# Plain float32 products in the first token block, weight splits after the last conversion, and a new order of the attention's small products

## The chip, the cores and the metric

The kernel runs on one core of a Trainium2 chip. The metric is device microseconds (us) from start to end of one execution: 2131.81 us is the median of three runs of the kernel before (2130.74 to 2133.03).

## The reference, cut to what matters

Three layers run one behind the other on 4 sequences of 768 tokens (3072 tokens, 384 features).

```python
# 1. gated linear attention, 8 heads of 48: for every token t
state = f[t][:, None] * state + outer(k[t], v[t])     # f = sigmoid(f_logit)
y[t] = q[t] @ state
# 2. first MoE (one dense expert), w_in 384 x 2048, w_out 2048 x 384; weights arrive as float64
x2 = square(maximum(y @ w_in, 0)) @ w_out
# 3. second MoE: 8 experts of width 1024, Sinkhorn-normalised gates P (8 rounds)
out = sum(P[:, e:e+1] * (maximum(x2 @ w1[e], 0) @ w2[e]) for e in range(8))
```

All results are float32. A product of two float32 matrices can be made in two ways on TensorE: "plain", with both operands as float32; or "split", where each operand is cut into a rounded part (type float32r, `hi`) and a rest (`lo = a - hi`), and three float32r products hi·hi, hi·lo and lo·hi are added up in PSUM.

## The kernel before, in words

Tokens are worked in 24 chunks of 128 (`c`), three chunks to a block of 384 (`blk` for attention, `j` for the first MoE), eight blocks. The first MoE has 16 slices `f` of 128 hidden features. Its step number is `i = 16 j + f`.

**Attention, per chunk.** Scans over the forget gates on DVE (`scan_r`, `scan_f`, L316 to L325), products with k and q on POOL (`mul_k` L328, `mul_q` L331), scores on TensorE (`scores` L344), the causal mask on DVE (L349), transposition and state update (`k_turn` L354, `state_in` L366), and the output `y` (`mix`): for each of four pairs of heads `p`, two products of the masked scores with v (L383; 128 rows, 64 columns of the array each, the left half for head `j=0`, the right for `j=1`), and, except for the first chunk of a sequence, two products of the old state with q (L386; rows and columns 64j to 64j+63 of the array). The order is pair after pair, L383 L383 L386 L386. All of them write one PSUM bank. ACT then copies `y` to the hi part of `x1` (`yh`, L417), DVE makes the lo part (`yl`, L415). In block 0 the fourth pair's output is spread to the other three by a product with a shift matrix (L404).

**Weights of the first MoE.** Each of the 16 slices comes from memory as 128 x 768 float64 words (`ldw`, into one of four buffers) and is converted to float32 by `cva` and `cvw` on ACT (L930, L933), three `cvb` steps on DVE (L937, L941, L945) and `cvs` on POOL (L949). Right behind that it is split: `cvh` on ACT (L280) writes the hi part, `cvl` (L283) the lo part, on DVE for ten of the slices and on POOL for six. A conversion buffer (`cvt`, three of them) is free again after `cvl`.

**First MoE, per step i.** `e1` (L499): nine float32r products of 128x128 by 128x384 (three feature tiles, three terms each). ACT: `r` (relu, L504), `sq` (square, L507), `hi` (L511). DVE: `lo` (L515). Then `e2` (L525): nine float32r products into three accumulators. `e2(i)` is due two steps behind `e1(i)`. Two PSUM buffers hold the results of `e1`, so `e1(i)` needs `r(i-2)`.

**Order.** Nothing is ordered by hand: `Plan.order` (L65 on) is a list scheduler. Every step has an engine, a cost in us, a due time in units of `i`, and the steps that it needs. The result is one order per engine, and each engine runs its queue strictly in that order. Conversions are due at `n - 4` and start no earlier than 14 + 3.5 n us of the planner's own clock. While no work is there at the start, `keep_warm` fills TensorE with products of the identity matrix (L245).

The second MoE follows (L678 first products, L729 second products); its prepared weights rotate through the ten slots of `wpool`, which before held slices 0 to 9 of the first MoE.

Of the kernel before, what the change touches and what calls it, by code (L numbers as in the profile page):

```python
# [20 lines left out]
NP = H // 2  # L21
# [32 lines left out]
LO_DVE = (4, 6, 8, 9, 10, 11, 12, 13, 14, 15)  # L54
# [96 lines left out]
def body(tc, fkq, v, wm, wa, wc, gate, seqs, out):  # L151
# [5 lines left out]
    wpool = ctx.enter_context(tc.tile_pool(name="wpool", bufs=NWP))  # L157
# [23 lines left out]
    wb = rpool("wb", NF - NWP)  # L181
# [82 lines left out]

    def new_w(n):
        W[n] = (wb if n >= NWP else wpool).tile([128, 2, WCOL], F32R, tag="w", name="w")
        return W[n]

    def ldw(n):
        if n in early:  # L270
            early[n] = early[n - 4] if n >= 4 else wb.tile([128, WCOL], I64, tag="w", name="raw64")
        raws[n] = early[n] if n in early else rawp.tile([128, WCOL], I64, tag="raw", name="raw64")
        sp.dma_start(out=raws[n], in_=wm[n])
# [101 lines left out]
    def new_y(c):  # L375

        tmp["y", c] = (ps_p if c >= CPB else ps_acc).tile([128, NP, CH], F32, tag="pp" if c >= CPB else f"a{1 + c % 2}", name="y")

    def mix_pair(c, p, rows=64):
        y, vv, kk, st = tmp["y", c], vt[c % 3], kq[c % 3], Sh.get(c)  # L380
# [3 lines left out]
        if st is not None:  # L384
            for j in range(2):
                pe.matmul(y[64 * j:64 * j + rows, p, :], st[64 * j:64 * j + DH, p, 0:rows], kk[64 * j:64 * j + DH, 1, p, :], start=False, stop=True)  # L386

    def mix(c):
        new_y(c)
        for p in range(NP):  # L390
            mix_pair(c, p)
        Psb.pop(c)


    def mix_last(c):
        new_y(c)
        mix_pair(c, NP - 1)

    def last_out(c):
        act.copy(out=ylast, in_=tmp["y", c][:, NP - 1, :])  # L400

    def mix_rest(c):
        for p in range(KD):
            pe.matmul(tmp["y", c][:, p, :], shift[:, 16 * p:16 * p + 128], ylast, start=True, stop=True)  # L404
            mix_pair(c, p, DH)
        Psb.pop(c)

    def y_part(c, lo):
        blk, t0 = c // CPB, (c % CPB) * CH
        if blk not in x1:  # L410
            x1[blk] = x1p.tile([128, 2, NP, BT], F32R, tag="x1", name="x1")
        n = NP if blk else KD
        hi, y = x1[blk][:, 0, 0:n, t0:t0 + CH], tmp["y", c][:, 0:n, :]
        if lo:
            dve.tensor_tensor(out=x1[blk][:, 1, 0:n, t0:t0 + CH], in0=y, in1=hi.bitcast(F32), op=ALU.subtract)  # L415
        else:
            act.copy(out=hi, in_=y)  # L417
# [7 lines left out]
    for c in range(NCH):  # L425
# [40 lines left out]
        needs = [("cm0", c), ("cm1", c), ("ldv", c), if_(not first, ("sh", c)), if_(1 < c < CPB, ("yl", c - 2))]  # L466
        if blk:
            at("mix", "pe", 2.1 if not first else 1.1, 2.5, mix, needs)
# [6 lines left out]
        at("yl", "dve", 0.62 if blk else 0.5, 3, lambda c: y_part(c, 1), [("yh", c)])  # L475
# [13 lines left out]
    add("conv", "none", 0, 0, close_conv, [("cvl", n) for n in range(NF)])  # L489
# [4 lines left out]
    def products_in(i, w, xx):  # L494
        ps = eps[i] = ps_e.tile([128, BT], F32, tag="e1", name="e1")
        n = 0
        for k in range(KD):
            for wl, xl in ((0, 0), (0, 1), (1, 0)):
                pe.matmul(ps, w[:, wl, k * 128:(k + 1) * 128], xx[:, xl, k, :], start=n == 0, stop=n == 3 * KD - 1)  # L499
                n += 1  # L500

    def m_relu(i):
        hl[i] = [hp.tile([128, BT], F32, tag="g", name="g", bufs=2)]
        act.activation(out=hl[i][0], in_=eps.pop(i), func=ACTF.Relu)  # L504
# [12 lines left out]
    def m_out(i):  # L517
        j, f = divmod(i, NF)
        _, hi, lo = hl.pop(i)
        w = W[f]  # L520
        if f == 0:
            acc1[j] = [ps_acc.tile([128, BT], F32, tag=f"a{m}", name=f"a{m}") for m in range(KD)]
        for m in range(KD):
            for n, (wl, g) in enumerate(((0, hi), (1, hi), (0, lo))):
                pe.matmul(acc1[j][m], w[:, wl, D + m * 128:D + (m + 1) * 128], g, start=f == 0 and n == 0, stop=f == NF - 1 and n == 2)  # L525
        if j == NB - 1:
            W.pop(f)
# [17 lines left out]
    E1, E2 = 1.49, 1.49  # L545
# [4 lines left out]
    for i in range(n1):  # L550
        j, f = divmod(i, NF)
        add(("e1", i), "pe", E1, i, lambda i=i: products_in(i, W[i % NF], x1[i // NF]),
            [("yl", q) for q in range(CPB) if i == 0] + [if_(j == 0, ("cvl", f)), if_(f == 0 and j, ("sprd", j)), if_(i, ("e1", i - 1)), e_free(i)])
        add(("r", i), "act", 0.42, i + 0.4, lambda i=i: m_relu(i), [("e1", i), if_(i >= 2, ("lo", i - 2))])
        add(("sq", i), "act", 0.45, i + 0.4, lambda i=i: m_square(i), [("r", i)])
        add(("hi", i), "act", 0.45, i + 0.4, lambda i=i: m_hi(i), [("sq", i), if_(i >= 3, ("e2", i - 3))])
        add(("lo", i), "dve", 0.5, i + 0.4, lambda i=i: m_lo(i), [("hi", i)])
        add(("e2", i), "pe", E2, i + LAG + 0.1, lambda i=i: m_out(i),
# [235 lines left out]
    for g in range(NSTEP):  # L794
# [125 lines left out]
class F64:  # L920
# [79 lines left out]
def general_path(ctx: ExitStack, tc: tile.TileContext, seqs, wm, wa, wc, gate, out):  # L1000
# [27 lines left out]
    with tc.tile_pool(name="g_a", bufs=2) as ap, tc.tile_pool(name="g_s", bufs=3) as sp_, \  # L1028
            tc.tile_pool(name="g_y", bufs=2 * hb, space=PSUM) as py, tc.For_i(0, B, 1) as b:
        for p in range(NP):  # L1030
# [17 lines left out]
            for h in range(hb):  # L1048
                t = ap.tile([128, BT], F32, name="g_yo")
                act.copy(out=t, in_=y[h])  # L1050
                for j in range(2):
                    if p < KD:
                        sp.dma_start(out=x1v[bass.ds(b, 1), h, 64 * j:64 * j + DH, p].rearrange("o p t -> (o p) t"), in_=t[64 * j:64 * j + DH, :])
                    else:
                        for kt in range(KD):
                            sp.dma_start(out=x1v[bass.ds(b, 1), h, 64 * j + DH:64 * j + 64, kt].rearrange("o p t -> (o p) t"),
                                         in_=t[64 * j + 16 * kt:64 * j + 16 * kt + 16, :])
# [85 lines left out]
def lay_out(inputs):  # L1143
# [16 lines left out]
    for kt in range(KD):  # L1160
        rows += [2 * kt * DH + r for r in range(DH)]
        rows += [6 * DH + 16 * kt + r for r in range(16)]
        rows += [(2 * kt + 1) * DH + r for r in range(DH)]
        rows += [7 * DH + 16 * kt + r for r in range(16)]
# [27 lines left out]
```

## Time and profile before

| | |
|---|---|
| median of 3 runs | 2131.81 us |
| profiled execution | 2132.19 us |
| its span (first to last instruction) | 2130.4 us |
| TensorE busy / granted clock over the span | 98% / 0.990 of full speed |
| DVE, ACT, POOL busy | 62%, 42%, 30% |

The span and the profiled execution's time differ by 1.8 us. Busy shares are averages over very different stages: attention and first MoE run to about 590 us, the second MoE from there to the end. So the views of single stretches count here, not the averages.

### The profile page before, as it was taken

The page shows a single profiled execution, that of the slowest core. Times are in us where ns is not written, and L with a number is a line of the kernel's source. Part 1 is how long each engine was busy: PE and PEld are TensorE (multiplying, and loading weights), DVE is VectorE, ACT ScalarE, POOL GpSimd, SP SyncE. Part 2 cuts the span into 40 slices and gives each one's busy share as a digit, 9 for nine tenths or more (in the row PEclk, how much of TensorE's full clock was granted, in tenths as well). Part 3 has the DMA queues.
Part 4 walks back from the last instruction along what each step waited for, and adds up shares of the span by engine and source line. Part 5 has one row for each costly group of instructions (what it writes and reads, how often), then busy time and mean ns, then how long its engine had stood idle before and what let it go on. Part 6 is the DMA issues. An engine that isn't in the chain of part 4 may idle for free.

```text
span 2130.4 us, 27837 instructions
## 1 busy us (share of the span) xinstructions
PE 2080.0 (98%) x10686; PEld 1762.8 (83%) x10686; DVE 1325.2 (62%) x2022; ACT 886.4 (42%) x1505; POOL 638.1 (30%) x636
## 2 busy tenths in 40 slices
PE   7889999999999999999999999999999999999998
PEld 5789899998987888878878888888887888888886
DVE  8973443332477666657677666756767766766674
ACT  4754444454643433423434433433433433443341
POOL 4531100010103333333332333334233243333331
PEclk9899999999999999999999999999999999999999
DMA  7342212110203111112122112121213111211210
GB/s 269 127 128 65 77 67 83 57 49 7 81 31 91 55 55 60 55 55 70 55 86 88 55 55 70 55 62 52 68 62 108 61 59 52 69 55 55 70 45 32
DMA packets 55114, 148.76 MB, mean 70 GB/s; under 512 B 6332, under 2 KB 15548, under 8 KB 54972
## 3 DMA queue, kind: packets, MB, share of 16 engines
q1 hardware_dynamic: 54972, 146.90, 21.6%
q8 instruction: 85, 1.39, 0.3%
q14 instruction: 57, 0.47, 0.1%
HBM read 135.28 MB, written 9.54 MB: 68 GB/s over the span
## 4 chain that ended last, share of the span: by engine, by line
PE 90%; DVE 6%; issue 1%; DMA 1%; POOL 1%; ACT 0%; SPq 0%; DVEq 0%; POOLq 0%; ACTq 0%
PE o L729 35%; PE e L678 33%; PE e L499 9%; PE a L525 8%; PE y L383 1%; PE y L386 1%; PE pp L344 1%; DVE cv_t L937 1%; DVE cv_t L945 1%; PE lg L540 1%; DVE lo L515 1%; PE ds L366 0%; DVE cv_t L941 0%; DVE w L283 0%; DVE sg L318 0%
## 5 line engine op out<-in xcount | busy, mean ns | idle before, releaser
L729 PE MATMUL o<-h,w 128*128 128x512 f32 x3456 | 792.8, 389 | 0.0
L729 PEld LDWEIGHTS o<-h,w 128*128 128x128 f32 x3456 | 648.1, 188 | 135.6 <-DVE sc L752 0.7
L678 PE MATMUL e<-x,w 128*128 128x512 f32 x3168 | 734.6, 391 | 10.4 <-DVE t L700 5.3
L678 PEld LDWEIGHTS e<-x,w 128*128 128x128 f32 x3168 | 597.2, 189 | 137.5 <-DVE t L700 7.0
L696 ACT COPY s<-e 128x512 f32<-128x512 f32 x288 | 168.9, 586 | 836.1 <-PE e L678 831.4
L761 POOL TENSOR_TENSOR acc<-acc,sc 128x512 f32<-128x512 f32 x258 | 334.4, 1303 | 536.4 <-DVE sc L752 529.5
L752 DVE TENSOR_TENSOR sc<-o,pb 128x512 f32<-128x512 f32 x264 | 182.0, 690 | 372.3 <-PE o L729 339.1
L718 DVE SCALAR_TENSOR_TENSOR h<-v,h 128x512 fp32r<-128x512 f32 x384 | 275.3, 736 | 1.8 <-ACT h L713 1.3
L713 ACT ACTIVATE h<-v 128x512 fp32r<-128x512 f32 x384 | 242.2, 631 | 52.8 <-DVE v L705 52.6
L705 DVE TENSOR_TENSOR v<-e,s 128x512 f32<-128x512 f32 x288 | 198.0, 688 | 74.7 <-ACT w L663 56.5
L650 POOL TENSOR_TENSOR rawa<-rawa 128x256 f32<-128x256 f32 x96 | 81.1, 845 | 537.4 <-DMA rawa<-in_wa_dram 347.8
L499 PE MATMUL e<-x,w 128*128 128x384 f32 x1152 | 229.0, 342 | 9.7 <-DVE w L283 6.2
L499 PEld LDWEIGHTS e<-x,w 128*128 128x128 f32 x1152 | 200.6, 190 | 16.7 <-DVE w L283 7.8
L515 DVE TENSOR_TENSOR lo<-g,hi 128x384 fp32r<-128x384 f32 x128 | 83.3, 653 | 208.6 <-ACT hi L511 208.6
L525 PE MATMUL a<-hi,w 128*128 128x384 f32 x768 | 200.1, 341 | 0.0
L667 DVE TENSOR_TENSOR w<-rawa,w 128x768 fp32r<-128x768 f32 x192 | 157.8, 823 | 8.1 <-ACT w L663 8.1
L663 ACT CAST w<-rawa 128x768 fp32r<-128x768 f32 x192 | 135.2, 728 | 29.6 <-DMA rawa<-in_wa_dram 12.4
L525 PE MATMUL a<-lo,w 128*128 128x384 f32 x384 | 131.0, 341 | 11.8 <-DVE lo L515 11.7
L525 PEld LDWEIGHTS a<-hi,w 128*128 128x128 f32 x768 | 140.3, 191 | 1.5 <-issue 0.3
L504 ACT ACTIVATE g<-e 128x384 f32<-128x384 f32 x128 | 62.9, 491 | 179.6 <-PE e L499 163.2
L328 POOL TENSOR_TENSOR kq<-kq,sg 128x512 f32<-128x512 f32 x24 | 30.9, 1287 | 290.7 <-DVE sg L318 161.6
L667 DVE TENSOR_TENSOR w<-rawc,w 128x768 fp32r<-128x768 f32 x96 | 92.5, 964 | 2.1 <-ACT w L663 2.0
(103 smaller groups left out, 1313.1 us busy)
## 6 DMA issues: line engine op xcount, KB each, us to landing
rawa<-in_wa_dram SPq DMA_DIRECT2D x96, 384.0 KB, 3.0
rawc<-in_wc_dram SPq DMA_DIRECT2D x96, 384.0 KB, 3.4
raw<-in_wm_dram SPq DMA_DIRECT2D x16, 768.0 KB, 6.2
pb<-ptd SPq DMA_DIRECT2D x24, 512.0 KB, 3.7
fraw<-in_fkq_dram SPq DMA_DIRECT2D x23, 512.0 KB, 4.0
kq<-in_fkq_dram SPq DMA_DIRECT2D x23, 512.0 KB, 4.6
vt<-in_v_dram SPq DMA_DIRECT2D x24, 192.0 KB, 5.0
x2d<-x2t SPq DMA_DIRECT2D x8, 576.0 KB, 2.8
```

The costliest lines, as they stand in the source:

```text
L499: pe.matmul(ps, w[:, wl, k * 128:(k + 1) * 128], xx[:, xl, k, :], start=n == 0, stop=n == 3 * KD - 1)
L525: pe.matmul(acc1[j][m], w[:, wl, D + m * 128:D + (m + 1) * 128], g, start=f == 0 and n == 0, stop=f == NF - 1 and n == 2)
L663: act.copy(out=W2[g, k][:, 0, 0:n], in_=src)
L667: dve.tensor_tensor(out=W2[g, k][:, 1, 0:n], in0=src, in1=W2[g, k][:, 0, 0:n].bitcast(F32), op=ALU.subtract)
L678: pe.matmul(ps, w[a], x[b], start=start and n == 0, stop=stop and n == 2, skip_group_check=True)
L696: act.copy(out=snap[g, n], in_=bank[g, "a"])
L705: dve.tensor_tensor(out=vs[g, k], in0=bank[g, k], in1=other, op=ALU.add)
L713: act.activation(out=hs[g // 2, t, f][:, 0], in_=vs[g, k], func=ACTF.Relu)
L718: dve.scalar_tensor_tensor(out=h[:, 1], in0=vs[g, k], scalar=0.0, in1=h[:, 0].bitcast(F32), op0=ALU.max, op1=ALU.subtract)
L729: pe.matmul(ob[q, t, m], w[:, a, c:c + 128], h[:, b], start=f == 0 and n == 0, stop=f == 3 and n == 2)
L752: dve.tensor_tensor(out=dst, in0=ob[q, t, m], in1=pbt[p, e][:, t * TB:(t + 1) * TB], op=ALU.mult)
L761: eng.tensor_tensor(out=acc[p, t, m], in0=acc[p, t, m], in1=sc[q, t, m], op=ALU.add)
```

## The change: what it does

- **First block plain.** For `j == 0`, `e1` and `e2` are three plain float32 products each, with the unsplit converted weights `R[n]`. `hi` and `lo` of the hidden values and `yl` of the first block fall away for these 16 steps. The planner's cost is 1.95 for such a step, 1.56 for the others (1.49 before).
- **Splits later.** `cvs` writes its sum to `R[n]`, 16 buffers of their own, so that a conversion buffer is free after `cvs`. `cvh` of every slice needs `cvs(15)`, the last conversion, and is due 16 steps later than before; `cvl` is on DVE for all 16 slices. Slices 8 to 13 are split into the space of `R[0]` to `R[11]`, and their `cvh` also needs `e2` and `cvl` of the two slices that lie there. `e1(16 + f)` needs `cvl(f)`.
- **Quarters.** `y` lies in two PSUM banks, even pairs in one, odd pairs in the other; for odd pairs the two heads swap halves of the columns. `mix` goes by two pairs at a time: four L383 products, then four L386 products, which lie on the four quarters of the array. `yh` and `yl` are two instructions of half the size each. In block 0 the new places hold, but the order stays pair after pair, and both banks are used by each chunk, so that chunk c waits for chunk c-1's copy.
- The rows of `w_in` are permuted on the host to fit. Slots of `wpool` are named; slots 8 and 9 now hold slices 14 and 15, so that the second MoE's weights come into these two slots after `e2` of steps 126 and 127. A DMA scratch size is set to 1024.

```diff
+    R = {}
+    PAIR_AT = {n: n for n in range(8)} | {14: 8, 15: 9}
+
+    def left_by(n):
+        return [] if n in PAIR_AT else [2 * (n - 8), 2 * (n - 8) + 1]
...
+    def cv_total(n):
+        R[n] = wb.tile([128, WCOL], F32, tag=f"b{n}", name="r")
+        F64(nc, cvt[n], raws[n]).total(R[n])
+
     def cv_hi(n):
-        act.copy(out=new_w(n)[:, 0, :], in_=cvt[n])
+        new_w(n)
+        act.copy(out=W[n][0], in_=R[n])
 
     def cv_lo(n):
-        (dve if n in LO_DVE else pool).tensor_tensor(out=W[n][:, 1, :], in0=cvt[n], in1=W[n][:, 0, :].bitcast(F32), op=ALU.subtract)
+        dve.tensor_tensor(out=W[n][1], in0=R[n], in1=W[n][0].bitcast(F32), op=ALU.subtract)
...
-        add(("cva", n), "act", 0.74, due, lambda n=n: cv_abs(n), [("ldw", n), if_(n >= 3, ("cvl", n - 3))], start=CV_AT + CV_STEP * n)
+        add(("cva", n), "act", 0.74, due, lambda n=n: cv_abs(n), [("ldw", n), if_(n >= 3, ("cvs", n - 3))], start=CV_AT + CV_STEP * n)
...
-        add(("cvs", n), "pool", 1.78, due, lambda p=part: p("total"), [("cvb", n, 2), ("cvw", n)])
-        add(("cvh", n), "act", 0.74, due, lambda n=n: cv_hi(n), [("cvs", n), if_(n >= NF - 2, ("cvs", n - 4))])
-        add(("cvl", n), *(("dve", 0.88) if n in LO_DVE else ("pool", 1.78)), due, lambda n=n: cv_lo(n), [("cvh", n)])
+        add(("cvs", n), "pool", 1.9, due, lambda n=n: cv_total(n), [("cvb", n, 2), ("cvw", n)])
+        gone = [(s, k) for k in left_by(n) for s in ("e2", "cvl")] + ([("cvs", n - 4)] if n >= 14 else [])
+        add(("cvh", n), "act", 0.8, due + NF, lambda n=n: cv_hi(n), [("cvs", NF - 1)] + gone)
+        add(("cvl", n), "dve", 0.95, due + NF, lambda n=n: cv_lo(n), [("cvh", n)])
...
+    def mix_in(c, p, rows=64):
+        vv, st = vt[c % 3], Sh.get(c)
+        y, n = y_at(c, p)
         for j in range(2):
-            h = 2 * p + j
-            pe.matmul(y[64 * j:64 * j + rows, p, :], vv[:, h * DH:h * DH + rows], Psb[c][:, j, p, :], start=True, stop=st is None)
...
+            h, o = 2 * p + j, 64 * (j ^ (p & 1))
+            pe.matmul(y[o:o + rows, n, :], vv[:, h * DH:h * DH + rows], Psb[c][:, j, p, :], start=True, stop=st is None)
...
     def mix(c):
         new_y(c)
-        for p in range(NP):
-            mix_pair(c, p)
+        for p in range(0, NP, 2):
+            for f in (mix_in, mix_state):
+                for i in range(2):
+                    f(c, p + i)
...
+        if i < NF:
+            for k in range(KD):
+                pe.matmul(ps, R[i][:, k * 128:(k + 1) * 128], xx[:, 0, k, :], start=k == 0, stop=k == KD - 1)
+            return
...
+            if j == 0:
+                pe.matmul(acc1[j][m], R[f][:, D + m * 128:D + (m + 1) * 128], g, start=f == 0, stop=f == NF - 1)
+                continue
...
+        dur = 1.56 if j else 1.95
+        add(("e1", i), "pe", dur, i, lambda i=i: products_in(i, W.get(i % NF), x1[i // NF]),
+            [("yl", q) for q in range(CPB) if i == 0] + [if_(j == 0, ("cvs", f)), if_(j == 1, ("cvl", f)), if_(f == 0 and j, ("sprd", j)), if_(i, ("e1", i - 1)), e_free(i)])
+        add(("r", i), "act", 0.42, i + 0.4, lambda i=i: m_relu(i), [("e1", i), if_(i >= 2, ("lo", i - 2)), if_(3 <= i < NF, ("e2", i - 3))])
...
-                free = ("e2", n1 - NF + n + NWP)
+                free = ("e2", n1 - NF + {v: k for k, v in PAIR_AT.items()}[n + NWP])
```

## Rows read from the trace of the kernel before

**Rows 1.** The page's second part: TensorE's busy tenths in 40 slices of 53 us.

```profile
PE   7889999999999999999999999999999999999998
```

**Rows 2.** Busy time by stretch: us, PE, PEld, DVE, ACT, POOL, clock, DMA share, GB/s.

```profile
34.00:147.00 113.00, 90.15 (x561) 78.15 (x561) 107.01 (x128) 68.33 (x112) 60.70 (x35) 0.89 0.44 143
147.00:590.00 443.00, 443.00 (x3192) 410.23 (x3192) 172.24 (x320) 219.58 (x407) 45.12 (x39) 1.00 0.19 62
```

**Rows 3.** TensorE's waits, 33 to 147 us: us in total, times, longest.

```profile
PE a L525 <- DVE lo L515: 11.7, 4, 8.5
PE e L499 <- DVE w L283: 6.2, 3, 3.2
```

**Rows 4.** Groups by line and shape, 22 to 130 us.

```profile
L949 POOL TENSOR_TENSOR cv_t<-cv_t,raw 128x768 int32<-128x768 int32 x16 | 33.6, 2097 | 36.0 <-DVE cv_t L945 17.7 <-ACT hi L511 6.7 <-issue 5.1
L515 DVE TENSOR_TENSOR lo<-g,hi 128x384 fp32r<-128x384 f32 x14 | 13.5, 982 | 0.0
L283 POOL TENSOR_TENSOR w<-cv_t,w 128x768 fp32r<-128x768 f32 x6 | 13.0, 2172 | 5.8 <-ACT w L280 5.8
L283 DVE TENSOR_TENSOR w<-cv_t,w 128x768 fp32r<-128x768 f32 x9 | 10.6, 1174 | 0.0
```

**Rows 5.** Timeline of DVE: start, length, line, operation.

```profile
30.91 2.06 DVE L941 TENSOR_SCALAR cv_t<-cv_t 128x768 int32<-128x768 int32 x1
80.35 0.94 DVE L283 TENSOR_TENSOR w<-cv_t,w 128x768 fp32r<-128x768 f32 x1
84.82 0.56 DVE L941 TENSOR_SCALAR cv_t<-cv_t 128x768 int32<-128x768 int32 x1
142.35 0.56 DVE L515 TENSOR_TENSOR lo<-g,hi 128x384 fp32r<-128x384 f32 x1 [1.00 <-ACT hi L511]
```

**Rows 6.** Timeline of POOL: an early split, and the last conversion.

```profile
30.32 2.23 POOL L283 TENSOR_TENSOR w<-cv_t,w 128x768 fp32r<-128x768 f32 x1 [3.62 <-ACT w L280]
...
127.30 2.36 POOL L949 TENSOR_TENSOR cv_t<-cv_t,raw 128x768 int32<-128x768 int32 x1 [2.24 <-DVE cv_t L945]
```

**Rows 7.** Timeline of ACT: `r(13)`, then `cva(15)`.

```profile
119.33 0.49 ACT L504 ACTIVATE g<-e 128x384 f32<-128x384 f32 x1 [0.89 <-PE e L499]
...
121.20 0.90 ACT L930 ACTIVATE cv_t<-raw 128x768 f32<-128x768 f32 x1 [0.27 <-DMA raw<-in_wm_dram]
```

**Rows 8.** Timeline of TensorE: first product of the MoE, plain identity products, the next.

```profile
34.08 0.42 PE L499 MATMUL e<-x,w 128*128 128x384 f32 x1
...
37.54 2.62 PE L245 MATMUL warm<-shift 128*128 128x128 f32 x22
39.91 3.65 PE L499 MATMUL e<-x,w 128*128 128x384 f32 x18
```

**Rows 9.** The chain that ended last: start, length, what.

```profile
145.37 1.56 PE e L499 x9
146.93 1.91 PE lg L540 x18
```

**Rows 10.** Products done, 33 to 147 us: L499, then L525 (columns as in Rows 2).

```profile
33.00:147.00 114.00, 38.76 (x180) 32.91 (x180) 0.90 0.44 144
33.00:147.00 114.00, 35.11 (x153) 30.39 (x153) 0.90 0.44 144
```

**Rows 11.** Timeline of TensorE, 150 to 168 us: `mix` of chunks 6 and 7.

```profile
150.87 1.09 PE L383 MATMUL y<-Psb,vt 128*64 128x128 f32 x16
151.79 0.62 PE L366 MATMUL ds<-vt,Kn 128*64 128x48 f32 x16
...
155.67 1.16 PE L344 MATMUL pp<-kq 48*128 48x128 f32 x16
...
164.16 0.40 PE L383 MATMUL y<-Psb,vt 128*64 128x128 f32 x4
...
167.06 1.14 PE L499 MATMUL e<-x,w 128*128 128x384 f32 x5
```

**Rows 12.** Timeline of the weight loads, 164 us.

```profile
164.49 0.20 PEld L386 LDWEIGHTS y<-kq,Sh 48*64 48x64 f32 x4 [0.17 <-issue]
```

More of the change, by code (lines that the diff above doesn't have):

```diff
@@ L263, in before @@
         return n - 4 if n in early else late[late.index(n) - 2] if late.index(n) > 1 else -1
+    R = {}
+    PAIR_AT = {n: n for n in range(8)} | {14: 8, 15: 9}
+    def left_by(n):
+        return [] if n in PAIR_AT else [2 * (n - 8), 2 * (n - 8) + 1]
     def new_w(n):
[L266 to L267 removed]
+        if n in PAIR_AT:
+            t = wpool.tile([128, 2, WCOL], F32R, tag=f"w{PAIR_AT[n]}", name="w")
+            W[n] = [t[:, l, :] for l in range(2)]
+        else:
+            W[n] = [wb.tile([128, WCOL], F32R, tag=f"b{k}", name="w") for k in left_by(n)]
     def ldw(n):
         if n in early:
[L271 removed]
+            early[n] = early[n - 4] if n >= 4 else wpool.tile([128, WCOL], I64, tag=f"w{8 + n % 2}", name="raw64")
         raws[n] = early[n] if n in early else rawp.tile([128, WCOL], I64, tag="raw", name="raw64")
@@ L375, in new_y, with y_at, mix_state @@
     def new_y(c):
-        tmp["y", c] = (ps_p if c >= CPB else ps_acc).tile([128, NP, CH], F32, tag="pp" if c >= CPB else f"a{1 + c % 2}", name="y")
-    def mix_pair(c, p, rows=64):
-        y, vv, kk, st = tmp["y", c], vt[c % 3], kq[c % 3], Sh.get(c)
-        for j in range(2):
-            h = 2 * p + j
-            pe.matmul(y[64 * j:64 * j + rows, p, :], vv[:, h * DH:h * DH + rows], Psb[c][:, j, p, :], start=True, stop=st is None)
-        if st is not None:
-            for j in range(2):
-                pe.matmul(y[64 * j:64 * j + rows, p, :], st[64 * j:64 * j + DH, p, 0:rows], kk[64 * j:64 * j + DH, 1, p, :], start=False, stop=True)
+        for n in range(2):
+            tmp["y", c, n] = (ps_p if c >= CPB else ps_acc).tile([128, NP, CH], F32, tag="pp" if c >= CPB else f"a{1 + n}", name="y")
+    def y_at(c, p):
+        return tmp["y", c, p % 2], p // 2
+    def mix_in(c, p, rows=64):
+        vv, st = vt[c % 3], Sh.get(c)
+        y, n = y_at(c, p)
+        for j in range(2):
+            h, o = 2 * p + j, 64 * (j ^ (p & 1))
+            pe.matmul(y[o:o + rows, n, :], vv[:, h * DH:h * DH + rows], Psb[c][:, j, p, :], start=True, stop=st is None)
+    def mix_state(c, p, rows=64):
+        kk, st = kq[c % 3], Sh.get(c)
+        y, n = y_at(c, p)
+        for j in range(2):
+            o = 64 * (j ^ (p & 1))
+            if st is not None:
+                pe.matmul(y[o:o + rows, n, :], st[64 * j:64 * j + DH, p, 0:rows], kk[64 * j:64 * j + DH, 1, p, :], start=False, stop=True)
     def mix(c):
         new_y(c)
-        for p in range(NP):
-            mix_pair(c, p)
+        for p in range(0, NP, 2):
+            for f in (mix_in, mix_state):
+                for i in range(2):
+                    f(c, p + i)
         Psb.pop(c)
@@ L396, in mix_last @@
         new_y(c)
-        mix_pair(c, NP - 1)
+        mix_in(c, NP - 1)
+        mix_state(c, NP - 1)
     def last_out(c):
-        act.copy(out=ylast, in_=tmp["y", c][:, NP - 1, :])
+        act.copy(out=ylast, in_=tmp["y", c, 1][:, 1, :])
     def mix_rest(c):
         for p in range(KD):
-            pe.matmul(tmp["y", c][:, p, :], shift[:, 16 * p:16 * p + 128], ylast, start=True, stop=True)
-            mix_pair(c, p, DH)
+            y, n = y_at(c, p)
+            pe.matmul(y[:, n, :], shift[:, 16 * p:16 * p + 128], ylast, start=True, stop=True)
+            mix_in(c, p, DH)
+            mix_state(c, p, DH)
         Psb.pop(c)
@@ L410, in y_part @@
         if blk not in x1:
[L411 to L417, printed above, removed]
+            x1[blk] = x1p.tile([128, 2, NP, BT], F32R if blk else F32, tag="x1", name="x1")
+        parts = [(slice(n, NP if blk else KD, 2), tmp["y", c, n][:, 0:2 - (n and not blk), :]) for n in range(2)]
+        for n, y in parts:
+            hi = x1[blk][:, 0, n, t0:t0 + CH]
+            if blk == 0:
+                act.copy(out=hi, in_=y)
+            elif lo:
+                dve.tensor_tensor(out=x1[blk][:, 1, n, t0:t0 + CH], in0=y, in1=hi.bitcast(F32), op=ALU.subtract)
+            else:
+                act.copy(out=hi, in_=y)
     def spread(blk):
@@ L465, in body @@
             at("sh", "dve", 0.35, 0, shat, [("st", c - 1), ("scanr", c), if_(c % NCB > 2, ("mix", c - 2))])
-        needs = [("cm0", c), ("cm1", c), ("ldv", c), if_(not first, ("sh", c)), if_(1 < c < CPB, ("yl", c - 2))]
+        needs = [("cm0", c), ("cm1", c), ("ldv", c), if_(not first, ("sh", c)), if_(0 < c < CPB, ("yl", c - 1))]
         if blk:
-            at("mix", "pe", 2.1 if not first else 1.1, 2.5, mix, needs)
+            at("mix", "pe", 1.5 if not first else 0.95, 2.5, mix, needs)
         else:
@@ L487, in close_conv @@
         pools["x2t"] = rpool("x2p", 2)
-    add("conv", "none", 0, 0, close_conv, [("cvl", n) for n in range(NF)])
+    add("conv", "none", 0, 0, close_conv, [("cvs", n) for n in range(NF)])
     hl, x2t, x2, eps = {}, {}, {}, {}
@@ L518, in m_out @@
         j, f = divmod(i, NF)
-        _, hi, lo = hl.pop(i)
-        w = W[f]
+        g, *parts = hl.pop(i)
         if f == 0:
@@ L523, in m_out @@
         for m in range(KD):
+            if j == 0:
+                pe.matmul(acc1[j][m], R[f][:, D + m * 128:D + (m + 1) * 128], g, start=f == 0, stop=f == NF - 1)
+                continue
+            hi, lo = parts
             for n, (wl, g) in enumerate(((0, hi), (1, hi), (0, lo))):
-                pe.matmul(acc1[j][m], w[:, wl, D + m * 128:D + (m + 1) * 128], g, start=f == 0 and n == 0, stop=f == NF - 1 and n == 2)
+                pe.matmul(acc1[j][m], W[f][wl][:, D + m * 128:D + (m + 1) * 128], g, start=f == 0 and n == 0, stop=f == NF - 1 and n == 2)
         if j == NB - 1:
@@ L1160, in lay_out @@
     for kt in range(KD):
[L1161 to L1164, printed above, removed]
+        for j in range(2):
+            rows += [(2 * kt + (j ^ (kt & 1))) * DH + r for r in range(DH)]
+            rows += [(7 - j) * DH + 16 * kt + r for r in range(16)]
     w_in = inputs["moe_w_in"][np.array(rows)]
```

40 lines of the change are left out of this document (21 added, 19 removed).

## The prediction

> **What bounds the kernel now.** I read the busy tenths first: TensorE is full in every slice but the first three or four [rows 1]. A table of stretches sharpens this: from 147 to 590 us TensorE is busy for 443.0 of 443 us at clock 1.00, while DVE and ACT have half their time free; from 34 to 147 us it has 90.15 of 113 us, at a granted clock of 0.89 (part of the time at the lower level, 1.2 GHz), and there DVE is the full engine with 107.01 [rows 2]. So there are two regimes. Behind 147 us one us of TensorE work taken away is one us won. Ahead of it the waits decide, and they name DVE: the lo part of the hidden values 11.7 us, the lo part of the weights 6.2 us [rows 3].
>
> DVE is not full of work, though. L941 takes 0.56 us at 84.82 and 2.06 us at 30.91, where POOL's L283 is running until 32.55 [rows 5, 6]. The longer one ends when POOL's ends: two instructions that the two engines can't run at the same time. The groups show the same as a mean: the hidden lo part has 982 ns for an instruction that takes 560 when alone [rows 4, 5]. In this stretch DVE and POOL together act nearly as one engine.
>
> **The change, part by part.** All of it is set against the profiled execution (2132.19 us).
>
> *1. The conversions end earlier.* The last `cvs` ends at 127.30 + 2.36 = 129.7 us [rows 6]. Taken off the DVE/POOL pair before that: 14 hidden lo parts, 6 splits on POOL, 9 on DVE; busy 13.5 + 13.0 + 10.6 = 37.1 us [rows 4]. A part of this is one waiting for the other. With 0.56 us for a lo part [rows 5], 0.94 for a DVE split [rows 5] and the POOL splits at their 2.17 [rows 4] it is 7.8 + 8.5 + 13.0 = 29.3 us. Not all of that lay on the pair's path (POOL waited 17.7 us for L945 alone [rows 4]); I take nine tenths, 26.5. So the last conversion ends at C = 103 us. Bounds: everything counts, 129.7 - 37.1 = 93; only what DVE loses counts (7.8 + 8.5), 113. That a conversion buffer is freed by `cvs` instead of `cvl`, and so the float64 loads on SP's queue can go earlier, lies inside these bounds. The moved steps issue no DMA.
>
> *2. What the plain products cost.* No plain product of 384 columns is in the trace. The nearest row: 22 instructions, which are 11 identity products of 128 columns, go from 37.54 to 39.91, 0.215 us each at full clock [rows 8]. Three times the columns make 0.645, three products 1.94 us a step. From below: nine float32r instructions of 384 columns take 1.56 us, 0.173 each [rows 9]; a plain product is two instructions, so no less than 0.35, or 1.04 a step. From above, with the 2.62 us that the group shows as busy, 2.14 a step. I take 1.94, from the row that is also plain. Against 1.56 [rows 9] that is 0.38 more for each of 32 steps, 12 us. It is paid on TensorE, in place of time in which TensorE now waits.
>
> *3. ACT's queue.* `cvh(0)` waits for `cvs(15)`, and behind it in ACT's queue stand the `r` of all later steps. Which ones, the order tells. In the kernel before `r(13)` stands ahead of `cva(15)` [rows 7], because the planner counted the DVE work that now goes. After the change the planner can start `cva(15)` at 66.5 of its clock and has `cvs(15)` at about 75. TensorE, from 32 on with 3.9 a slice and two chunks of attention at 3.4, then stands at slice 9. I use this for the order only. So `r(0)` to `r(9)` are ahead of `cvh(0)` and `r(10)` is behind. On the chip TensorE can do `e1` up to 11 and `e2` up to 9, and then has to wait for C. This wait is new, and it takes the place of the ones in [rows 3].
>
> *4. The end of the front.* To compare at the same state: by 146.93 the kernel before has done 20 `e1` and 17 `e2` (180 and 153 products of nine each [rows 10]), all of block 0's and block 1's attention, and chunk 6's scores. After C there remain ten plain steps (`e1(12..15)`, `e2(10..15)`), 19.4 us; `mix` of chunk 5, 2.9, and the scores of chunk 6, 1.1 to 1.2 [rows 11], 4.0; five split steps of block 1, 7.8; and some 1.8 us for a stretch at the lower clock level after the wait (zero if TensorE never waits long; at most the 10 us that ten plain steps would take extra at half the clock). Together 33, so C + 33 = 136 instead of 147: 11 us won. By the bounds of C, 126 to 146: 21 to 1 us.
>
> *5. The splits.* 16 ACT copies, by the planner's cost of 0.8 us, and 16 DVE subtractions of 0.94 [rows 5], 28 us on two engines, between C and block 1, whose `e1(16+f)` needs them one by one. ACT and DVE are free for half of the time there [rows 2], so I cost them at nothing. Were that cover gone, the first would be late by its own 1.7 us and each next one by nothing, since a step pair lasts 3.1 us. Between ACT's `r` they can cost up to 0.8 us each, hidden by the two PSUM buffers.
>
> *6. The quarters.* `mix` of chunk 6, eight L383 products and no state, takes 151.79 - 150.87 = 0.92 us, 0.115 a product. `mix` of chunk 7, eight and eight, takes 167.06 - 164.16 = 2.90, not 1.84 [rows 11]. The 1.06 more goes with the seven changes of kind inside it: at each the weight loads stand still for 0.17 us [rows 12]. So a change costs 0.15. Now there are three instead of seven, and the one to the next work remains: 0.6 won per chunk. Against it, the second and third L383 product of each four now share a half of the columns, where before neighbours never did. At most this brings each of these products from 0.115 to 0.16: 0.36 lost. I take 0.5 won. It counts for the 15 chunks of blocks 2 to 7 that have a state, since there TensorE is full: 7.5 us, with bounds 0.2 x 15 = 3 and 0.95 x 15 = 14 (products also at half their time, see the rival). For the three first chunks of a sequence I take nothing; the loss would be 1 us.
>
> *7. Small parts.* `yh` and `yl` in two halves cost ACT and DVE a second start per chunk, beside full TensorE and in their free half [rows 2]; block 0's `yl` goes. Slots 8 and 9 come free for the second MoE six slices later, just before its start; they are for its third and fourth weight steps, which are not needed by then, so I cost it at nothing, or at one pair of steps, 3.1 us, if TensorE has to wait behind ACT's queue there. The second MoE is the same otherwise.
>
> **Sum.** 11 + 7.5 = 18.5 us: 2132.2 - 18.5 = 2113.7; the median of the runs lies 0.4 below the profiled execution. Forecast 2113.5 us, its own range 2107 to 2121.
>
> **The rivals.**
>
> *TensorE becomes the bound of the front too* (14%). The conversions run ahead as far as the bound of 93, and ACT's queue doesn't hold `r` back. Then from 34.1 us on TensorE does, without a gap, 32 x 1.94 = 62, three chunks at 4.6 (1.16 and 0.62 [rows 11], 2.4, and 0.4 for the transposition) = 14, and 7.8 + 1.1: it is there at 119 instead of 147, 28 us won, with the quarters 35.5: 2096.5. For it: waits for DVE are what it has now. Against: part 3.
>
> *Four quarters at once* (12%). The state products would also halve, from 0.115 to 0.058, 8 x 0.058 x 15 = 7 more: 2106.5. Against it speaks that each product is two instructions on the same quarter one behind the other, and that chunk 6's eight products with two halves reach just two at a time. The Trainium skill, "TensorEngine Tiling (Array Packing)", section "Tiling Modes", has the 64x64 mode as four independent tiles and says that tiles operate independently; by that rule the state products would gain up to twofold over today's two tiles. No row here has four of them at a time.
>
> *The quarters bring nothing* (14%): neighbours on the same columns eat what fewer changes give. 2121.
>
> *The conversions don't end earlier* (7%): the slower side. Their pace is set not by the DVE/POOL pair but by ACT's queue, in which each `cva(n)` stands behind an `r(k)` that waits for TensorE's now longer steps. Then C stays near 130, the front ends at 163 instead of 147, 16 lost, with the quarters 8.5: 2140.7. It decides from C above 121.5. Against it: ACT is busy for 68.33 of the 113 us and DVE for 107.01 [rows 2].
>
> *Near that point* (7%): C of 119 to 124, no change that shows.
>
> **How the numbers follow.** The forecast has 46%. Of no change a measurement can tell about 0.2%, 4.3 us. Faster: 46 + 14 + 12 + 14 = 86%; within 0.2%: 7%; slower: 7%. The range from 2098 to 2125 leaves out half of the first rival and the last two.
>
> **What would show it.** Last L949 at 103 (93 to 113). ACT standing at the first L280 until then, and TensorE with an L499 behind it. Plain L499 products at 0.65 us each. Logits of block 0 (L540) near 136. In `mix`, 2.4 us per chunk with state, four groups instead of eight. TensorE without a gap from there to the second MoE, which keeps its length. It is wrong if the last conversion is past 115, if L283 shows up among TensorE's waits in block 1, or if `mix` stays at 2.9.

## The result, and the profile after

The changed kernel takes 2105.37 us (median of 4 runs, 2104.01 to 2106.93) against 2132.42 for the kernel before on the same chip: a ratio of 0.9874, interval 0.9857 to 0.9891. The forecast was 2113.5, its whole range 2098 to 2125; the time lies below the likeliest case's own range (2107 to 2121). The profiled execution took 2106.04 us, its span 2104.3, 26.1 less than before.

One instruction cuts the span well: the first of the 18 logit products of a block (`lg`). The timeline of TensorE of the kernel before has block 0's and block 7's so (the chain of [rows 9], another view, has 146.93 for the first; here all starts are taken from timelines):

```profile
146.77 2.07 PE L540 MATMUL lg<-gate_sb,x2t 128*128 128x8 f32 x18
...
593.30 2.46 PE L540 MATMUL lg<-gate_sb,x2t 128*128 128x8 f32 x18
```

The same engine's timeline after the change (start, length, engine, line, operation; in square brackets the idle time ahead and what ended it). L540 and L569 are the new plain products, L544 and L573 the split ones, L408 and L416 what was L383 and L386 (the two kinds of products in `mix`), L588 the logits:

```profile
70.96 2.10 PE L540 MATMUL e<-x,r 128*128 128x384 f32 x6
72.90 2.10 PE L569 MATMUL a<-g,r 128*128 128x384 f32 x6
...
107.21 3.00 PE L540 MATMUL e<-x,r 128*128 128x384 f32 x6 [2.21 <-ACT g L549]
110.00 3.01 PE L569 MATMUL a<-g,r 128*128 128x384 f32 x6
112.85 2.10 PE L540 MATMUL e<-x,r 128*128 128x384 f32 x6
...
133.59 2.07 PE L588 MATMUL lg<-gate_sb,x2t 128*128 128x8 f32 x18
...
150.98 0.62 PE L408 MATMUL y<-Psb,vt 128*64 128x128 f32 x8
151.53 0.45 PE L416 MATMUL y<-kq,Sh 48*64 48x128 f32 x8
151.91 0.66 PE L408 MATMUL y<-Psb,vt 128*64 128x128 f32 x8
152.50 0.45 PE L416 MATMUL y<-kq,Sh 48*64 48x128 f32 x8
152.88 1.83 PE L544 MATMUL e<-x,w 128*128 128x384 f32 x9
...
564.95 2.46 PE L588 MATMUL lg<-gate_sb,x2t 128*128 128x8 f32 x18
```

| part of the span | before | after | won | forecast |
|---|---|---|---|---|
| start to block 0's logits | 146.8 | 133.6 | 13.2 | 11 |
| block 0's to block 7's logits | 446.5 | 431.4 | 15.2 | 7.5 |
| block 7's logits to the end | 1537.1 | 1539.3 | -2.2 | 0 |

The last line is not the change: in the other executions profiled here this part took 1532.8 to 1541.6 us whatever the edit, and the unaltered changed kernel, profiled once more, had 1537.2. So the front came out near its forecast, and the quarters gave twice theirs.

The two stretches of [rows 2], the second now ending at 563 (same columns), of the kernel after:

```profile
34.00:147.00 113.00, 101.64 (x553) 68.12 (x553) 101.45 (x132) 67.04 (x111) 51.38 (x30) 0.95 0.44 152
147.00:563.00 416.00, 416.00 (x3084) 393.68 (x3083) 169.50 (x323) 212.35 (x412) 46.26 (x39) 1.00 0.19 62
```

Ahead of 147 us TensorE is busy for 11.5 us more and the granted clock rose from 0.89 to 0.95; DVE is still nearly full. Behind 147 us, up to block 7's logits, TensorE has no gap in either kernel. Its waits from 33 to 147 us (total, times, longest), against [rows 3]:

```profile
PE pp L360 <- DVE x L453: 5.9, 2, 5.5
PE e L540 <- ACT g L549: 2.2, 1, 2.2
```

In the kernel before, the wait of the first of these lines was

```profile
PE pp L344 <- DVE x L415: 1.2, 1, 1.2
```

The waits for the lo parts are gone. The longest now has grown from 1.2 us: chunk 4's scores (L360) wait for chunk 3's `yl` (L453), which stands in DVE's queue behind conversions and scans.

### The profile page after: what moved, and what is told of

It is laid out like the page before. It is cut to its first block, busy times and chain, and to the rows that moved or that the text cites. A ratio compares the mean times of both kernels' runs of the same rounds, so it can differ in the third digit from the quotient of the medians.

```text
span 2104.3 us, 27584 instructions
## 1 busy us (share of the span) xinstructions
PE 2063.2 (98%) x10558; PEld 1733.9 (82%) x10558; DVE 1316.3 (63%) x2030; ACT 878.6 (42%) x1513; POOL 629.6 (30%) x630
## 4 chain that ended last, share of the span: by engine, by line
PE 91%; DVE 4%; issue 1%; DMA 1%; POOL 1%; ACT 1%; SPq 0%; DVEq 0%; POOLq 0%; ACTq 0%
PE o L780 36%; PE e L729 33%; PE e L544 9%; PE a L573 8%; PE pp L360 1%; PE y L408 1%; PE lg L588 1%; PE y L416 1%; DMA rawa<-in_wa_dram 1%; DVE cv_t L992 1%; PE ds L382 1%; PE a L569 1%; DVE cv_t L996 0%; PE ktr L370 0%; DVE sg L334 0%
## 5 line engine op out<-in xcount | busy, mean ns | idle before, releaser
L729 PEld LDWEIGHTS e<-x,w 128*128 128x128 f32 x3168 | 597.2, 189 | 137.9 <-ACT s L747 7.7
L544 PE MATMUL e<-x,w 128*128 128x384 f32 x1008 | 198.1, 339 | 0.0
L560 DVE TENSOR_TENSOR lo<-g,hi 128x384 fp32r<-128x384 f32 x112 | 65.4, 584 | 199.5 <-ACT hi L556 198.9
L544 PEld LDWEIGHTS e<-x,w 128*128 128x128 f32 x1008 | 174.0, 188 | 4.8 <-issue 2.4
L573 PE MATMUL a<-hi,w 128*128 128x384 f32 x672 | 171.7, 336 | 0.0
L573 PEld LDWEIGHTS a<-hi,w 128*128 128x128 f32 x672 | 120.6, 188 | 0.9
L573 PE MATMUL a<-lo,w 128*128 128x384 f32 x336 | 112.4, 335 | 0.0
```

The costliest lines, as they stand in the source:

```text
L544: pe.matmul(ps, w[wl][:, k * 128:(k + 1) * 128], xx[:, xl, k, :], start=n == 0, stop=n == 3 * KD - 1)
L573: pe.matmul(acc1[j][m], W[f][wl][:, D + m * 128:D + (m + 1) * 128], g, start=f == 0 and n == 0, stop=f == NF - 1 and n == 2)
L729: pe.matmul(ps, w[a], x[b], start=start and n == 0, stop=stop and n == 2, skip_group_check=True)
```

## Experiments

Two theories go with the front: **loads** (the last conversion at 112.9 instead of 103 because ACT stands for the last two float64 loads) and **DVE** (because DVE's queue is full of other work until then). For the quarters: **changes** (only the fewer changes of kind pay) and **four at once** (the four state products of a group run together). Each run is named with its median and its ratio to the kernel before, and C is the end of its last conversion.

**The plain block and the late splits alone** (`e1_oldmix`): the changed kernel with the old `mix`.

```diff
-        for p in range(0, NP, 2):
-            for f in (mix_in, mix_state):
-                for i in range(2):
-                    f(c, p + i)
+        for p in range(NP):
+            mix_in(c, p)
+            mix_state(c, p)
...
-            h, o = 2 * p + j, 64 * (j ^ (p & 1))
+            h, o = 2 * p + j, 64 * j
```

(One bank, whole copies, the old order of the rows of `w_in` and the old costs of `mix` come back too.)

> The changed kernel with the old mix: one PSUM bank, heads not swapped, pair after pair, whole copies. What is left is the plain first block and the late splits. From the two traces the part between the first and the last logits of the first MoE gave 15.0 us, the part ahead of it 13.3. Theory A (all of the middle part is the quarters): 2105.4 + 15 = 2120, mix of a chunk with state back at 2.9 us. My prediction's size for the quarters (7.5): 2113. Rival (the quarters also helped the front, whose three chunks were in TensorE's way): 2123.

2121.8 us, 0.9953 (0.9936 to 0.9970). Timeline of TensorE, the two logit starts:

```profile
137.78 2.07 PE L581 MATMUL lg<-gate_sb,x2t 128*128 128x8 f32 x18
...
584.25 2.46 PE L581 MATMUL lg<-gate_sb,x2t 128*128 128x8 f32 x18
```

The stretch between is 446.5 as before the change; what is won lies ahead of it, and there 9.0 us of the 13.2 are left.

**The quarters alone** (`e2_quarters`): the kernel before, with the part of the diff that belongs to the quarters (two banks, swapped halves, halved copies, the rows of `w_in`, the costs of `mix`, and the order below).

```diff
-        for p in range(NP):
-            mix_pair(c, p)
+        for p in range(0, NP, 2):
+            for f in (mix_in, mix_state):
+                for i in range(2):
+                    f(c, p + i)
```

> The kernel before with the quarters alone: two banks, heads swapped, two pairs at a time, halved copies; the first block split as before. Theory A (worth 1.0 us for each of 15 chunks where TensorE is full, nothing ahead of 147 us): 2132 - 15 = 2117, mix 1.90 instead of 2.90. Rival (halved copies cost DVE in the front, which is full there): 2119 to 2121.

2117.36 us, 0.9934 (0.9918 to 0.9951). The same two rows:

```profile
147.04 2.07 PE L560 MATMUL lg<-gate_sb,x2t 128*128 128x8 f32 x18
...
577.62 2.46 PE L560 MATMUL lg<-gate_sb,x2t 128*128 128x8 f32 x18
```

The mirror image: the front stays at 147.0 (146.8 before), the stretch between shrinks to 430.6. The two halves won 10.5 and 15.0 us by the medians, both together 27.1; the 1.6 between is within the intervals.

**Pair after pair, banks and swap kept** (`e3_pairwise`).

```diff
-        for p in range(0, NP, 2):
-            for f in (mix_in, mix_state):
-                for i in range(2):
-                    f(c, p + i)
+        for p in range(NP):
+            mix_in(c, p)
+            mix_state(c, p)
```

> The changed kernel, banks and swapped heads kept, but mix pair after pair again: L408 L408 L416 L416, seven changes of kind in a chunk instead of three. Theory A1 (a change of kind costs some 0.15 us, and that is where the gain comes from): mix of a chunk near 2.5 to 2.9, 2115 to 2120. Theory A2 (two banks and swapped halves let products overlap whatever the order): mix stays near 1.9, 2105.

2116.69 us, 0.9925 (0.9909 to 0.9942), 446.5 between the logits. Timeline of TensorE, the `mix` of a chunk with state:

```profile
149.81 0.41 PE L408 MATMUL y<-Psb,vt 128*64 128x128 f32 x4
150.15 0.43 PE L416 MATMUL y<-kq,Sh 48*64 48x128 f32 x4
...
152.72 1.83 PE L543 MATMUL e<-x,w 128*128 128x384 f32 x9
```

From 149.81 to 152.72 are 2.91 us: behind the front, the new places win nothing by themselves. The front is 5.4 us shorter than in `e1_oldmix` (logits at 132.42 against 137.78). That is more than the 1.2 us by which the fronts of like programs differ here (under `e10_again`); which of banks, half copies or the planner's cost of `mix` does it was not tried.

**Two pairs at a time, but no swap** (`e4_noswap`): the group of four state products lies on two quarters instead of four.

```diff
-            h, o = 2 * p + j, 64 * (j ^ (p & 1))
+            h, o = 2 * p + j, 64 * j
```

(The same in `mix_state`, and the rows of `w_in` go with it.)

> The changed kernel, two pairs at a time and two banks kept, but the heads not swapped, so the four state products lie on two quarters instead of four. Theory A1 (only the changes of kind count): the group of four state products (L416 x8) stays at 0.38 us, the time at 2105 or, as neighbours no longer share columns, 1 to 2 us below. Theory A2 (four quarters at once): the group goes to 0.46 or more, while the group of L408 goes from 0.57 to 0.46; the sum near 2105 to 2107.

2111.79 us, 0.9911 (0.9895 to 0.9928), 437.5 between the logits.

```profile
149.74 0.62 PE L408 MATMUL y<-Psb,vt 128*64 128x128 f32 x8
150.29 0.65 PE L416 MATMUL y<-kq,Sh 48*64 48x128 f32 x8
150.88 0.66 PE L408 MATMUL y<-Psb,vt 128*64 128x128 f32 x8
...
152.05 1.83 PE L544 MATMUL e<-x,w 128*128 128x384 f32 x9
```

From 149.74 to 152.05 are 2.31 us. From start to start the L416 group takes 0.59 here and 151.91 - 151.53 = 0.38 in the changed kernel; the L408 group takes 0.55 to 0.59 in both. Both theories hold: fewer changes give 0.6 a chunk (2.91 to 2.31), four quarters 0.4 (2.31 to 1.90). Two banks are in both kernels; whether four quarters gain as much with one bank was not tried.

**The state products of both groups side by side** (`e8_abba`): the second two pairs begin with their state products, so that eight stand in a row.

```diff
-        for p in range(0, NP, 2):
-            for f in (mix_in, mix_state):
+        turn = c in Sh
+        for p, fs in ((0, (mix_in, mix_state)), (2, (mix_state, mix_in) if turn else (mix_in, mix_state))):
+            for n, f in enumerate(fs):
                 for i in range(2):
-                    f(c, p + i)
+                    f(c, p + i, second=n == 1 and turn)
```

(`second` puts `start` on the first product of a place and `stop` on the second.)

> The changed kernel; the second two pairs of mix take the state products first: L408 x8, L416 x8, L416 x8, L408 x8, so two changes of kind inside a chunk instead of three. From the runs so far a group of four state products costs 0.38 with a change of kind in it, and a change costs 0.147. Theory A1 (each change has its price): mix of a chunk with state from 1.91 to 1.76, 15 times, 2.2 us less, 2103. Rival (the eight state products in a row use the same quarters twice, so nothing is won): 2105.

2101.04 us (2096.91 to 2105.30), 0.9859 (0.9842 to 0.9876): faster than both kernels by its median, though its interval overlaps that of the changed kernel in the same comparison (`e10_again`, below: 0.9875, 0.9858 to 0.9891). The trace is sharper:

```profile
133.30 2.07 PE L589 MATMUL lg<-gate_sb,x2t 128*128 128x8 f32 x18
...
150.72 0.62 PE L408 MATMUL y<-Psb,vt 128*64 128x128 f32 x8
151.27 0.67 PE L416 MATMUL y<-kq,Sh 48*64 48x128 f32 x16
151.87 0.66 PE L408 MATMUL y<-Psb,vt 128*64 128x128 f32 x8
152.46 1.85 PE L545 MATMUL e<-x,w 128*128 128x384 f32 x9
...
562.39 2.46 PE L589 MATMUL lg<-gate_sb,x2t 128*128 128x8 f32 x18
```

1.74 us a chunk instead of 1.90, 429.1 between the logits instead of 431.4: 15 chunks by 0.16. The rest of the 3.8 us between the medians is probably not the edit's: of the 6.7 us between the two profiled executions 4.4 lie behind block 7's logits (1532.8 against 1537.2), where the programs are the same. Sixteen L416 instructions take 0.60 us and eight take 0.38: 0.22 for eight more, hence 0.055 a product and some 0.16 for the change of kind.

**A real wait for the last conversion** (`e5_truewait`): the first split reads one column of `R[15]` first.

```diff
+        if n == 0:
+            act.copy(out=W[0][0][:, 0:1], in_=R[NF - 1][:, 0:1])
```

> The changed kernel with one more ACT instruction ahead of the first split: it copies one column of the last converted slice, so that ACT really waits there for the last conversion. In the changed kernel the first L295 starts at 107.5 us, before the last conversion ends (112.9): the wait that the prediction built on isn't there. Theory W (such a wait would have cost what the prediction took it to): r of step 12 goes from 108 to 113.5, TensorE stands for some 3 to 5 us, 2108 to 2111. Rival (TensorE has other work until then): under 1 us, 2105 to 2106.

2105.53 us, 0.9873 (0.9856 to 0.9889): no difference that the medians show, with an interval of some 3.5 us to each side. The wait is there, on ACT:

```profile
113.35 0.19 ACT L296 CAST w<-r 128x1 fp32r<-128x1 f32 x1 [4.70 <-POOL r L1002]
```

and on TensorE behind it:

```profile
114.94 2.17 PE L542 MATMUL e<-x,r 128*128 128x384 f32 x6 [2.59 <-ACT g L551]
```

It is not free in this profile: block 0's logits start at 135.77, 2.2 and 2.4 us later than in the two profiles of the unaltered kernel (133.59, and 133.36 in `e10_again`), about the 2.59 us that TensorE idles here. A cost of that size the medians can't tell from none; the 3 to 5 us of idle time that were expected didn't come.

The changed kernel idles nearly as long ahead of 107.21 (2.21 us). In that profile the granted clock from 107 to 113 us is 0.72, a part of the stretch at 1.2 GHz, and two steps take 2.8 to 2.9 us instead of 1.94. In the unaltered kernel's second profile (`e10_again`, idle 2.10) the same stretch has 1.00, and so has the stretch from 113 to 119 us here, around the longer wait. So the lower clock there belongs to the execution, not to the wait's length.

**Eight splits early, on DVE** (`e6_early8`) and **on POOL** (`e9_early8pool`).

```diff
-        add(("cvh", n), "act", 0.8, due + NF, lambda n=n: cv_hi(n), [("cvs", NF - 1)] + gone)
-        add(("cvl", n), "dve", 0.95, due + NF, lambda n=n: cv_lo(n), [("cvh", n)])
+        add(("cvh", n), "act", 0.8, due if n < 8 else due + NF, lambda n=n: cv_hi(n), [("cvs", n if n < 8 else NF - 1)] + gone)
+        add(("cvl", n), "dve", 0.95, due if n < 8 else due + NF, lambda n=n: cv_lo(n), [("cvh", n)])
```

(For POOL: `cvl` of these eight on "pool", cost 1.9.)

> The changed kernel, but slices 0 to 7 are split right behind their own conversion, due n - 4, as in the kernel before; the others stay late (their space isn't free earlier). Theory S (DVE and POOL together set the pace, so eight splits of 0.94 us put the last conversion later by 8 to 10 us, and the front with it): 2110 to 2115. Rival (the front is set by loads and by TensorE, DVE has room): 2105 to 2107.

> The changed kernel, slices 0 to 7 split right behind their conversion, their lo part on POOL instead of DVE. With the lo parts on DVE (the run before) the last conversion went from 112.9 to 122.7 us and the time to 2110.2. Theory D (only DVE's queue sets the pace; POOL's splits find room): the last conversion stays within 3 us of 113, 2105 to 2107. Rival, which the prediction took (DVE and POOL together act as one engine): eight times 2.17 at nine tenths, the last conversion near 128, 2110 to 2118.

On DVE 2110.24 us, 0.9890 (0.9874 to 0.9907); on POOL 2110.89 us, 0.9904 (0.9888 to 0.9921). The last conversion, timeline of POOL, first in `e6_early8`, then in `e9_early8pool`:

```profile
119.88 2.86 POOL L1000 TENSOR_TENSOR r<-cv_t,raw 128x768 int32<-128x768 int32 x1 [2.14 <-DVE d L333]
```

```profile
119.08 2.87 POOL L1000 TENSOR_TENSOR r<-cv_t,raw 128x768 int32<-128x768 int32 x1 [2.14 <-ACT w L295]
```

C goes from 112.9 to 122.7 and to 122.0: 1.2 us for each split on DVE, 1.1 for each on POOL. These are net prices, since the planner moved other work too: ahead of the last `cvb` DVE has 16 scans in both runs and 18 in the changed kernel. Block 0's logits start at 141.04 and 142.85, 7.5 and 9.3 later. So a split counts on either engine; that only DVE's part counts, the bound of 113 in the forecast, is not how it works. In `e9_early8pool` the late front doesn't come through C, though: TensorE has no gap from 97.44 on there, and what it lost lies ahead of that, in waits for DVE's mask (L365: 7.4 us in all, against 2.1 in the changed kernel).

**The last two loads earlier** (`e7_loads4`): slices 14 and 15 get two of the early buffers.

```diff
-    early = {n: None for n in (2, 3, 6, 7, 10, 11)}
+    early = {n: None for n in (2, 3, 6, 7, 10, 11, 14, 15)}
```

(Slices 12 and 13 take the later buffers.)

> The changed kernel, but the last two float64 slices go into the two buffers of slices 10 and 11 instead of those of 12 and 13, so that their loads need not wait for conversions 12 and 13. In the changed kernel ACT waits 6.9 and 4.5 us for these two loads, with r of steps 10 and 11 behind them. Theory L (the late loads set the end of the conversions, and TensorE's gap of 2.2 us at 105 us and its slow clock behind it come from them): the last conversion at 103 to 106, 2101 to 2103. Rival (TensorE's own work sets the front by then): 2105.

2106.08 us, 0.9880 (0.9861 to 0.9899). In the changed kernel ACT stands for these loads; timeline of ACT there:

```profile
97.31 0.93 ACT L981 ACTIVATE cv_t<-raw 128x768 f32<-128x768 f32 x1 [6.90 <-DMA raw<-in_wm_dram]
...
104.47 0.90 ACT L981 ACTIVATE cv_t<-raw 128x768 f32<-128x768 f32 x1 [4.50 <-DMA raw<-in_wm_dram]
...
106.58 0.49 ACT L549 ACTIVATE g<-e 128x384 f32<-128x384 f32 x1
...
107.53 0.82 ACT L295 CAST w<-r 128x768 fp32r<-128x768 f32 x1
```

With the edit, again ACT, and then DVE at the last conversion:

```profile
98.77 0.92 ACT L981 ACTIVATE cv_t<-raw 128x768 f32<-128x768 f32 x1 [0.58 <-DMA raw<-in_wm_dram]
```

```profile
111.89 1.09 DVE L996 SCALAR_TENSOR_TENSOR cv_t<-raw,cv_t 128x768 int32<-128x768 int32 x1
```

The waits are gone, and the last `cvb` still comes at 111.89, C at 115.0, block 0's logits at 136.62. So the loads don't set C; what is left is DVE's queue. But they do set something. In the changed kernel's profile the chain of work that ended last doesn't pass the last conversion at all:

```profile
97.58 2.66 POOL r L1000
...
100.25 4.20 DMA raw<-in_wm_dram
...
106.69 0.38 ACT g L549
...
107.21 3.00 PE e L540 x6
```

POOL frees a buffer, the load of slice 15 comes, ACT works it off and then does `r`, TensorE starts, and from there on it has no gap. In the second profile (`e10_again`) and here the chain goes along DVE's queue instead, through the last conversions and the splits; in `e10_again` TensorE's last wait on it is 0.2 us. The two chains are thus nearly equally long, so shortening one of them, as this edit does, wins nothing.

**The changed kernel once more** (`e10_again`), nothing edited, beside `e8_abba` and `e9_early8pool`.

> The changed kernel once more, unaltered, as the control of this call and to see how far the front of one execution differs from another. Logits of block 0 in 133.6 plus or minus 2 us; 2105.

2104.86 us, 0.9875 (0.9858 to 0.9891); logits at 133.36 and 564.73, C 114.0. Block 0's logits start within 132.35 to 133.59 in it, in the first profile and in the two runs whose edit leaves the front nearly as it is (`e4_noswap`, `e8_abba`), with one profile each. Differences of about 1 us in the front are not read here.

## Why the prediction was right or wrong

The time fell into the stated range, but 1.6 us below the likeliest case's own; nearest to it lies the rival of four quarters at once (2106.5, given 12%), whose mechanism the runs show beside the forecast one. The gain ahead of block 0's logits came near its forecast partly by luck (step 4).

**Step 1, the conversions (failed in size).** Forecast C = 103, bounds 93 to 113; measured C = 112.9, at the far bound. Timeline of POOL of the changed kernel, the last conversion:

```profile
110.43 2.44 POOL L1000 TENSOR_TENSOR r<-cv_t,raw 128x768 int32<-128x768 int32 x1 [2.75 <-ACT w L295]
```

The row puts the wait ahead of it down to ACT. But DVE's last `cvb`, whose result the conversion reads, ends only at 110.30, just before the start:

```profile
109.34 0.96 DVE L996 SCALAR_TENSOR_TENSOR cv_t<-raw,cv_t 128x768 int32<-128x768 int32 x1
```

The share of nine tenths was wrong both ways: by the two early-split runs a split weighs, net, 1.2 us on DVE (0.85 assumed) and 1.1 on POOL (1.95 assumed). With these and the hidden lo parts as assumed, 9 x 1.2 + 6 x 1.1 + 7 = 24.4 us would go, C = 105. The other 8 us I can only partly name. (One reading behind this step was off: the L941 of [rows 5] ends at 32.97, 0.42 us behind POOL's L283 and not with it.) Groups by line, before the change from 22 to 130 us, then after it from 22 to 113 us (count, busy us and mean ns):

```profile
L318 DVE TENSOR_TENSOR_SCAN sg<-sg,d 128x516 f32<-128x516 f32 x5 | 10.4, 2081 | 0.2
...
L324 DVE TENSOR_TENSOR_SCAN sg<-sg,d 128x516 f32<-128x516 f32 x4 | 7.6, 1888 | 0.0
```

```profile
L334 DVE TENSOR_TENSOR_SCAN sg<-sg,d 128x516 f32<-128x516 f32 x6 | 11.7, 1956 | 0.6
...
L340 DVE TENSOR_TENSOR_SCAN sg<-sg,d 128x516 f32<-128x516 f32 x6 | 8.2, 1362 | 0.0
```

Twelve scans stand ahead of the last `cvb` where eight did (the ninth of the rows before starts at 128.01, the last `cvb` at 126.11): the planner filled the freed DVE time with the attention of two later chunks. Two of each are an estimated 6.6 us by the means after (1.96 and 1.36), and each chunk has an L341 of up to 1.75 us as well (below). That the scans are the cause was not tried; the early-split runs, where a chunk's two scans went behind the last `cvb` again, fit it.

**Step 2, the price of a plain product (right).** From the L540 at 70.96 to the L569 at 72.90 are 1.94 us, the value taken from the identity products.

**Step 3, the wait on ACT (failed).** "`cvh(0)` waits for `cvs(15)`" is what the planner's list says, but that list makes only the order; the instruction waits for the data it reads, `R[0]`, and starts at 107.53, while the last conversion runs until 112.87. What held back the `r` was something else ahead of them in the same queue: `cva(14)` and `cva(15)`, waiting for loads (6.90 and 4.50 us). TensorE lost 2.21 us to it. The order was misread too: not ten `r` but twelve, `r(0)` to `r(11)`, stand ahead of the first split, the last one at 106.58. So TensorE could do two more `e1` and two more `e2` ahead of C than forecast, wait or no wait, and when `e5_truewait` made the wait real, TensorE stood for only 2.59 us.

**Step 4, the end of the front (right by two errors).** C + 33 was forecast and C + 20.7 measured. Behind C, TensorE had six plain steps instead of ten (7.8 us less; the four are those that the two more `r` allow, in `e5_truewait` as well), `mix` of chunk 5 was already done (2.9), and there was no stretch at the lower clock (1.8): together 12.5, against the measured 33 - 20.7 = 12.3 less. C was 10 later, so 133.6 came out near 136. And in this profile C is not what the front's end hangs on (the chain under `e7_loads4`), so C + 20.7 is a sum and not a cause.

The forecast has no row for its term of 1.8 us at the lower clock. The changed kernel's profile has a cost of that size, but ahead of C: two steps from 107.21 to 112.85 take 5.64 us instead of 3.88. The second profile has none there. The bound of 10 us given for that term is too low by half: ten plain steps at half the clock would take 19 more.

**Step 5, the splits (right).** On DVE fourteen of them go in one row, at 1.2 us each instead of 0.94, and TensorE has no gap from 107.21 to block 7's logits (0.2 us in `e10_again`). Timeline of DVE of the changed kernel (the L341 are read at the end):

```profile
47.49 0.13 DVE L341 TENSOR_TENSOR minf<-minf,sg 128x4 f32<-128x4 f32 x1
...
98.50 1.75 DVE L341 TENSOR_TENSOR minf<-minf,sg 128x4 f32<-128x4 f32 x1
...
110.22 16.94 DVE L298 TENSOR_TENSOR w<-r,w 128x768 fp32r<-128x768 f32 x14
```

**Step 6, the quarters (right mechanism, size off by two).** 0.5 us a chunk was forecast; [rows 11] and 152.88 - 150.98 = 1.90 make it 1.0, for 15 chunks 15 us. The saving by fewer changes was right (0.6, `e4_noswap`). The loss set against it by L408 products that share columns doesn't exist (0.55 to 0.59 a group with and without). The rival of four quarters at once came on top of it: 0.38 instead of 0.59 a group, so with 0.15 for the change taken off, 0.057 a state product instead of 0.11. The Trainium skill, "TensorEngine Tiling (Array Packing)", section "Tiling Modes", has four independent 64x64 tiles; this trace now agrees, 0.057 with four against 0.11 with two (`e4_noswap`). That each product is two instructions on the same quarter, which the forecast held against it, did not prevent the gain. For chunks without a state nothing was forecast, and 0.93 us (L408 at 137.69, the next product at 138.62) is nothing (0.92 before [rows 11]).

**Step 7, small parts (right).** The second MoE's part (1539.3) lies within the spread of the variants of the changed kernel, none of which alters it (1532.8 to 1541.6).

## What to carry to other kernels

Where one engine is full without a gap, price a change by its work there, term by term, and check each term's sign: here one loss was feared that doesn't exist, and one gain left out that does. Where waits decide, look at what the order lets pass next into the time taken from the full engine (here four scans, a likely cause but not a tested one), and at the chain that ended last before one of several waits is called the cause. And a "need" in this planner is an order, not a wait: the first split started 5.3 us before the conversion that it "needs" had ended, since it reads another slice.

## What the runs showed of the hardware

A DVE instruction of only 128x4 elements takes 0.13 us at 47.49 and 1.75 us at 98.50: the second ends at 100.25, as POOL's L1000 does that runs from 97.58 to 100.24, and at 47.49 POOL stands still. So small size doesn't spare an instruction from a wait for POOL. Changing between the two shapes of products in `mix` costs about 0.15 us each time; state products come at 0.057 us each on four quarters, at 0.11 on two. And the same program showed a granted clock of 0.72 and of 1.00 in the same six us, with waits of 2.21 and 2.10 us.
